# Five opening steps of an attention and gated-convolution kernel: order on TensorE, and which engine casts what when

## The chip, the cores and the metric

One core of one Trainium2 chip runs the program. The metric is device time in microseconds (us); lower is better. The engines are named as in the profile: PE is TensorE's matmul, PEld its weight load, DVE is VectorE, ACT is ScalarE, POOL is GpSimd, SP is the queue that issues nearly all DMAs.

## The reference, cut to what matters

Batch 8, 8 heads, 576 positions, head dimension 64. Attention is causal by blocks of 64; its output, 512 wide, goes through a causal depthwise convolution of five taps, a sigmoid gate, and two 512 by 512 projections.

```python
scores = scale * np.matmul(q, k.transpose(0, 1, 3, 2))
mask = (pos[:, None] // 64) >= (pos[None, :] // 64)
attn = softmax(np.where(mask, scores, -1e9))
x = np.matmul(attn, v)            # heads laid side by side: 576 x 512
gate_pre = sum(conv_w[k] * x_shifted_by(4 - k) for k in range(5))
gate = 1.0 / (1.0 + np.exp(-gate_pre))
out = (gate * (x @ w_val)) @ w_out
```

All inputs and the output are float32 in HBM. The kernel computes in float16 with float32 accumulation, so each input is cast once on the chip.

## The kernel before

**Units of work.** The 64 (batch, head) pairs are taken two heads at a time: 32 steps, numbered p = 0 to 31, four to a batch. Of the 576 positions the first 512 are loaded per step; the last 64 of all heads of a batch (the "tail") are loaded and cast once for a batch. Names used below, with p a step and b a batch:

- `load_qk1(p)`, `load_v1(p)`, `load_tails(b)`, `load_vtail(b)`: DMAs into float32 staging tiles (`qks`, `vs`, `tlst`, `vtst`; four buffers each for the first two).
- `cast_qk(p)` (L130), `cast_v(p)` (L135), `cast_tails(b)` (L116), `cast_vtail(b)` (L119): casts to float16, on POOL after step 0.
- `trans(p)`: eight TensorE transposes of the cast Q and K (L156) into PSUM bank 2, then one DVE copy (L167) into `qkT`. This is the input transpose; step p needs the result of `trans(p)`.
- `s_tile(p, t)` for t = 0, 1, 2: score matmuls into one of two PSUM tiles named `S`, then an exponential on ACT (L190) into `pt`.
- `s_last(b)`: the scores of the tails of one batch, with an exponential on ACT (L200).
- `mask(p)`: two POOL memsets on `pt` (L206, L208) that zero what causality forbids; it needs the exponential of `s_tile(p, 2)`.
- `av(p, h, bank)`: 15 matmuls of `pt` by V for head h; `norm(p, h, bank)`: reciprocal and multiply on DVE (L237, L238) into `x16`. `avs` is `av`, `norm` for head 0 and then for head 1.
- `xtrans(p)`: five transposes of `x16` (L252), the output transpose, and a DVE copy (L254) into `xt`.
- `conv(n)`: 80 small matmuls and three tanh activations (L275, L278); `val`, `out_tile`: the two projections.
- `trans_tails(b)`: transposes of the cast tail (L142) and a DVE copy (L145).
- `cast_w_out(f)` (L394), `permute_w_out(x)`: the output weights are cast in two halves at steps 7 and 8 and permuted by small matmuls at steps 9 to 11.

**Order.** The order on each engine is the order of the statements, written out by hand; nothing reorders it. An engine takes its instructions strictly in that order and waits on semaphores for the others. Steps 0 to 4 are one loop (attention only), steps 5 to 31 a second loop, which adds the convolution and the projections of a step five earlier. In each step `loads(p)` is issued first (Q and K of step p + 4, V of step p + 3), then `casts(p)` (Q and K of step p + 1, V of step p), then the scores.

Two of the details that are touched: at step 6 the cast of batch 2's tail comes not with the other casts but after `mask(6)`, and from step 9 on `casts(p)` casts Q and K up to two steps ahead.

Of the kernel before, what the change touches and what calls it, by code (L numbers as in the profile page):

```python
# [10 lines left out]
def kernel(  # L11
# [10 lines left out]
    nc = tc.nc  # L22
# [5 lines left out]
    B, H, SEQ, D = q.shape  # L28
    NP = B * H // 2
    out2d = out.rearrange("b s n -> (b s) n")  # L30

    def mm(out, lhsT, rhs, start=True, stop=True):
        nc.tensor.matmul(out=out, lhsT=lhsT, rhs=rhs, start=start, stop=stop,  # L33
                         skip_group_check=True)
# [10 lines left out]
    def const(shape, dt, tag):  # L45
        return cpool.tile(shape, dt, tag=tag, name=tag)
# [7 lines left out]
    w_st2 = const([128, 4, 512], fp32, "w_st2")  # L54
    w16 = const([128, 4, 512], fp16, "w16")
# [16 lines left out]
    def gbank(i=None):  # L72
        if i is None:
            i = ring[0] % 4
            ring[0] += 1
        return GT[i]
# [3 lines left out]
    qk16, tl16, qkT, gv = {}, {}, {}, {}  # L80
# [32 lines left out]
    def cast_tails(b, eng):  # L113
        t = p2.tile([128, 8, 64], fp16, tag="tl16", name="tl16")
        tl16[b] = t
        eng.tensor_copy(out=t[0:128, 0:8, 0:64], in_=tl_st.pop(b)[0:128, 0:8, 0:64])  # L116

    def cast_vtail(b):
        nc.gpsimd.tensor_copy(out=v16t[b % 2][0:128, 0:8, 0:64], in_=vtst[b % 2][0:128])  # L119

    def cast_qk(p, first=False):
        t = p3.tile([128, 4, 4, 64], fp16, tag="qk16", name="qk16")
        qk16[p] = t
        s = qk_st.pop(p).rearrange("p i h (n d) -> p (i h) n d", n=4)
        o = t[0:128].rearrange("p n e d -> p e n d")
        if first:
            nc.vector.tensor_copy(out=o[:, 0:2], in_=s[:, 0:2])
            nc.vector.tensor_copy(out=o[:, 2:4], in_=s[:, 2:4])
        else:
            nc.gpsimd.tensor_copy(out=o, in_=s)  # L130

    def cast_v(p):
        b, g = divmod(p, 4)
        s = v_st.pop(p)
        nc.gpsimd.tensor_copy(out=v16s[p % NV][0:128, 0:4, 0:2, 0:64], in_=s)  # L135
# [13 lines left out]
    def trans(p, bank=None):  # L149
        t = qk16.pop(p)  # L150
        banks = (2, 0) if p == 0 else (bank, bank)
        rr = [GT[i][0:128].bitcast(fp16) for i in banks]
        for i in range(2):
            for c in range(4):
                o = 512 * i + 128 * c
                nc.tensor.transpose(out=rr[i][:, o:o + 128], in_=t[0:128, c, 2 * i:2 * i + 2, 0:64],  # L156
                                    identity=ident16[0:128, 0:128])
        src = [r.rearrange("p (i n s) -> p i s n", i=2, n=4) for r in rr]
        if p == 0:
            o = [const([128, 512], fp16, f"qk0_{i}")[0:128] for i in range(2)]  # L160
            nc.scalar.copy(out=o[0].rearrange("p (s n) -> p s n", n=4), in_=src[0][:, 0])
            nc.vector.tensor_copy(out=o[1].rearrange("p (s n) -> p s n", n=4), in_=src[1][:, 1])
            qkT[p] = o
        else:
            o = p3.tile([128, 2, 512], fp16, tag="qkT", name="qkT")
            qkT[p] = [o[0:128, i] for i in range(2)]
            nc.vector.tensor_copy(out=o[0:128].rearrange("p i (s n) -> p i s n", n=4), in_=src[0])  # L167
# [36 lines left out]
    def mask(p):  # L204
        pt = pts[p % NPT]
        nc.gpsimd.memset(  # L206
            pt[64:128, 0:2, 0:1536].rearrange("p h (t s) -> p h t s", t=3)[:, :, :, 0:64], 0.0)
        nc.gpsimd.memset(pt[64:128, 0:2, 896:960], 0.0)  # L208
# [6 lines left out]
    def av(p, h, bank):  # L215
        b, g = divmod(p, 4)
        pt = pts[p % NPT]
        vv = v16s[p % NV]
        r = gbank(bank)
        for i in range(5):  # L220
            for j in range(i + 1):
                if j == 4:
                    o = 64 * (4 * h + g)
                    l = pt4[b % 2][0:128].rearrange("p a s -> p (a s)")[:, o:o + 128]
                    w = v16t[b % 2][0:128, 2 * g + h, 0:65]
                else:
                    o = 1280 + 64 * j if i == 4 else off[j] + 128 * i
                    l = pt[0:128, h, o:o + 128]
                    w = vv[0:128, j, h, 0:65]
                mm(r[0:128, 65 * i:65 * i + 65], l, w, start=(j == 0), stop=(j == i))  # L230

    def norm(p, h, bank):
        if h == 0:
            x16[p] = p3.tile([128, 5, 2, 64], fp16, tag="x16", name="x16")
        O = GT[bank][0:128, 0:325].rearrange("p (i d) -> p i d", d=65)
        rc = p2.tile([128, 5, 1], fp32, tag="rc", name="rc")
        nc.vector.reciprocal(out=rc[0:128], in_=O[:, :, 64:65])  # L237
        nc.vector.tensor_tensor(  # L238
            out=x16[p][0:128, 0:5, h, 0:64], in0=O[:, :, 0:64],
            in1=rc[0:128].to_broadcast([128, 5, 64]), op=ALU.mult)  # L240

    def avs(p, banks):
        for h in range(2):
            av(p, h, banks[h])
            norm(p, h, banks[h])
# [106 lines left out]
    def warm(n, bank=1):  # L352
        for _ in range(n):
            mm(GT[bank][0:128, 0:512], wz[0:128, 0:128], wz[0:128])
# [36 lines left out]
            scalar1=0.5, scalar2=None, op0=ALU.mult)  # L391

    def cast_w_out(f):
        nc.gpsimd.tensor_copy(out=w16[0:128, 2 * f:2 * f + 2, 0:512],  # L394
                              in_=w_st2[0:128, 2 * f:2 * f + 2, 0:512])


    T_LOAD = {{1: 0, 2: 4, 3: 7}.get(b, 4 * b - 6): b for b in range(1, B)}
    T_CAST = {{1: 3, 2: 6, 3: 9}.get(b, 4 * b - 4): b for b in range(1, B)}
    T_TRANS = {{1: 3, 2: 7, 3: 10}.get(b, 4 * b - 4): b for b in range(1, B)}  # L400
    T_LAST = {{0: 0, 1: 4, 2: 8, 3: 12}.get(b, 4 * b - 2): b for b in range(B)}

# [16 lines left out]

    def casts(p):  # L420
        for i in (p + 1, p + 2):
            if i < NP and i not in qkT and i not in qk16 and (p >= 9 or i == p + 1):
                cast_qk(i)
        cast_v(p)
        if p % 4 == 0:
            cast_vtail(p // 4)
        if p in T_CAST and p != 6:
            cast_tails(T_CAST[p], nc.gpsimd)

    def mask_and_casts(p):  # L430
        mask(p)
        if p == 6:
            cast_tails(T_CAST[p], nc.gpsimd)
        if p in (7, 8):
            cast_w_out(p - 7)

    outs = []

# [11 lines left out]
    for p in range(LAG):  # L450
        loads(p)
        casts(p)
        s_tile(p, 0)
        s_tile(p, 1)
        if p == 0:
            warm(2)
            trans_tails(0, 0)
            s_tile(0, 2)
            mask(0)
            trans(1, 2)  # L460
            warm(2)
            s_last(0)
            conv_weights()
            continue
        if p > 1:
            xtrans(p - 2, 3)
        av(p - 1, 0, 0)
        norm(p - 1, 0, 0)
        av(p - 1, 1, 1)
        trans(p + 1, 2)  # L470
        norm(p - 1, 1, 1)
        s_tile(p, 2)
        mask_and_casts(p)
        if p == 1:
            warm(2, 3)
        if p in T_TRANS:
            trans_tails(T_TRANS[p], 0)
        if p == 4:
            s_last(1)

    for p in range(LAG, NP):
        gs = p - LAG
        cv = gs % 2 == 0
        early = p < 12
        h = gs - 1
        loads(p)
        casts(p)
        if p == 6:
            scale_w_val(0)
            scale_w_val(1)  # L490
        s_tile(p, 0)
        s_tile(p, 1)
        if p == LAG:
            xtrans(p - 2, 3)
        avs(p - 1, (0, 1) if cv else (1, 0))
        if p < NP - 1:
            trans(p + 1, 2)
        if not early:
            out(3)
        elif gs > 0:  # L500
            val(h // 2, 2 * (h % 2), 3)
        s_tile(p, 2)
        mask_and_casts(p)
        if p in T_LAST:
            s_last(T_LAST[p])
        if cv:
            conv(gs // 2, (0, 1), early)
        xtrans(p - 1, 2 if cv else 0)
        if gs > 0:
            if not early:  # L510
                val(h // 2, 2 * (h % 2), 3)
            val(h // 2, 2 * (h % 2) + 1, 3 if early and cv else 1 if early else 0 if cv else 2)
            if h % 2 == 1:
                complete(h // 2)
        if p == 6:
            scale_w_val(2)
            scale_w_val(3)
        if 9 <= p <= 11:
            permute_w_out({9: 0, 10: 1, 11: 3}[p], 2)
        if p == 10:  # L520
            permute_w_out(2, 3)
        if p in T_TRANS:
            trans_tails(T_TRANS[p], 2 if cv else 0 if early else 1)
# [47 lines left out]
```

## Time and profile before

| what | value |
|---|---|
| median of 13 runs | 198.33 us (197.55 to 200.39) |
| the profiled execution, its time | 197.85 us |
| its span, first to last instruction | 196.1 us |
| PE busy | 180.6 us, 92% |
| ACT busy | 137.8 us, 70% |
| DVE busy | 131.7 us, 67% |
| POOL busy | 82.9 us, 42% |
| granted TensorE clock | 1.00 |
| HBM traffic over the span | 203 GB/s |

The table is of one profiled execution; the span leaves out 1.75 us that the execution's own time has around it. Busy shares are averages over the whole span. The kernel has two regimes: up to about 55 us PE has holes, and from then to about 176 us it has none to speak of. The row of POOL looks light, but a queue that is idle half the time can still hand over each piece late.

### The profile page before, as it was taken

How to read it: one execution, taken by the hardware profiler on the slowest of the kernel's cores; microseconds unless marked ns; L12 is line 12 of the kernel's file. 1: busy time of each engine (PE TensorE's matmuls, PEld its weight loads, DVE VectorE, ACT ScalarE, POOL GpSimd, SP SyncE). 2: the span in 40 equal slices, each digit the busy share in tenths (PEclk: the TensorE clock that was granted, in tenths of full speed). 3: DMA queues.
4: the chain of work that ended last, by engine and by line, in shares of the span. 5: the costliest groups of instructions: out<-in, count | busy, mean ns of one | idle time of the engine just before them, and what ended most of it. 6: DMA issues, size and time to landing. Idle time of an engine off the chain costs nothing.

```text
span 196.1 us, 8701 instructions
## 1 busy us (share of the span) xinstructions
PE 180.6 (92%) x3700; PEld 123.2 (63%) x3700; DVE 131.7 (67%) x287; ACT 137.8 (70%) x191; POOL 82.9 (42%) x168
## 2 busy tenths in 40 slices
PE   3897878869899999999999999999999999999992
PEld 0474665656576577677667776767767676755550
DVE  5378778958668586768677768687776867542451
ACT  0777788647688888877887788887888797545321
POOL 7274775156944644455434543464445422100000
PEclk9999999999999999999999999999999999999999
DMA  6999999999999567778797688868774111144355
GB/s 167 268 284 263 249 322 315 219 264 233 294 198 274 165 201 198 210 224 238 202 261 233 188 241 226 231 193 245 219 216 110 57 57 57 59 159 155 130 207 214
DMA packets 70337, 40.43 MB, mean 206 GB/s; under 512 B 48149, under 2 KB 64789, under 8 KB 70298
## 3 DMA queue, kind: packets, MB, share of 16 engines
q1 hardware_dynamic: 68288, 39.07, 72.5%
q10 hardware_dynamic: 2010, 0.80, 1.8%
q8 instruction: 29, 0.48, 1.1%
q14 instruction: 10, 0.08, 0.2%
HBM read 30.42 MB, written 9.44 MB: 203 GB/s over the span
## 4 chain that ended last, share of the span: by engine, by line
PE 79%; DMA 10%; DVE 3%; POOL 2%; ACT 1%; issue 1%; SPq 1%; ACTq 0%; POOLq 0%; DVEq 0%
PE G L33 48%; PE S L33 18%; PE G L156 7%; DMA qks<-in_k_dram 6%; PE G L252 5%; DMA tlst<-in_k_dram 3%; DVE qkT L167 2%; POOL qk L130 2%; DMA vs<-in_v_dram 1%; PE G L142 1%; ACT L324 1%; POOL w L394 1%; DVE xt L254 0%; DVE gv L292 0%; SPq L95 0%
## 5 line engine op out<-in xcount | busy, mean ns | idle before, releaser
L190 ACT ACTIVATE pt<-S 128x1024 f16<-128x1024 f32 x96 | 94.9, 1024 | 23.4 <-PE S L33 21.1
L206 POOL MEMSET pt<- 64x384 f16 x32 | 13.2, 413 | 77.9 <-ACT pt L190 77.9
L167 DVE COPY qkT<-G 128x1024 f16<-128x1024 f16 x31 | 37.7, 1216 | 4.1 <-PE G L156 4.0
L33 PE MATMUL G<-xt,w_val 128*128 128x288 f16 x256 | 38.7, 286 | 0.4 <-issue 0.4
L292 DVE SCALAR_TENSOR_TENSOR gv<-th,G 128x288 f16<-128x288 f32 x64 | 28.2, 452 | 13.1 <-PE G L33 11.5
L33 PE MATMUL G<-w_out,gv 128*128 128x512 f16 x144 | 36.5, 379 | 0.0
L33 PEld LDWEIGHTS <-pt 128*128 128x128 f16 x960 | 31.5, 97 | 7.3 <-issue 5.1
L33 PE MATMUL G<-v,pt 128*128 128x65 f16 x896 | 34.0, 194 | 1.3 <-issue 0.8
L130 POOL CAST qk<-qks 128x1024 f16<-128x1024 f32 x31 | 32.3, 1043 | 5.0 <-DMA qks<-in_k_dram 3.3
L314 ACT COPY osb<-G 128x512 f32<-128x512 f32 x31 | 18.2, 587 | 22.2 <-PE G L33 19.5
L238 DVE TENSOR_TENSOR x<-G,rc 128x320 f16<-128x320 f32 x64 | 31.4, 491 | 2.2
L33 PE MATMUL S<-qkT 64*128 64x512 f16 (+1 forms) x248 | 28.7, 301 | 3.3 <-DVE qkT L167 1.9
L33 PEld LDWEIGHTS <-qkT 64*128 64x128 f16 x496 | 16.2, 94 | 23.7 <-issue 16.3
L33 PEld LDWEIGHTS <-w_val 128*128 128x128 f16 x256 | 23.9, 98 | 8.0 <-issue 0.6
L254 DVE COPY xt<-G 128x576 f16<-128x576 f16 x32 | 14.6, 457 | 15.1 <-PE G L252 14.8
L156 PE MATMUL G<-ident,qk 128*128 128x128 f16 x256 | 20.1, 222 | 4.6 <-POOL qk L130 2.7
L237 DVE RECIPROCAL rc<-G 128x5 f32<-128x5 f32 x64 | 12.1, 189 | 17.8 <-PE G L33 17.6
L135 POOL CAST v<-vs 128x512 f16<-128x512 f32 x32 | 20.7, 648 | 0.7 <-DMA vs<-in_v_dram 0.5
L33 PEld LDWEIGHTS <-gv 128*128 128x128 f16 x144 | 12.9, 98 | 9.9
L156 PEld LDWEIGHTS <-qk 128*128 128x128 f16 x256 | 15.1, 99 | 6.1 <-POOL qk L130 3.1
L33 PE MATMUL G<-xt,DG 32*32 32x288 f16 x640 | 16.9, 288 | 0.0
L33 PE MATMUL S<-xt,DG 32*32 32x288 f16 x640 | 16.7, 287 | 0.0
(58 smaller groups left out, 147.1 us busy)
## 6 DMA issues: line engine op xcount, KB each, us to landing
out_dram<-osb SPq DMA_DIRECT2D x35, 256.0 KB, 2.4
qks<-in_q_dram SPq DMA_DIRECT2D x32, 256.0 KB, 4.2
qks<-in_k_dram SPq DMA_DIRECT2D x31, 256.0 KB, 4.4
vs<-in_v_dram SPq DMA_DIRECT2D x62, 128.0 KB, 4.5
tlst<-in_q_dram SPq DMA_DIRECT2D x8, 128.0 KB, 4.5
vtst<-in_v_dram SPq DMA_DIRECT2D x8, 128.0 KB, 4.6
w_st<-in_moe_w_val_dram SPq DMA_DIRECT2D x2, 512.0 KB, 6.1
w_st<-in_moe_w_out_dram SPq DMA_DIRECT2D x2, 512.0 KB, 6.2
```

The lines of the kernel that those rows point to most:

```text
L33: nc.tensor.matmul(out=out, lhsT=lhsT, rhs=rhs, start=start, stop=stop, skip_group_check=True)
L130: nc.gpsimd.tensor_copy(out=o, in_=s)
L135: nc.gpsimd.tensor_copy(out=v16s[p % NV][0:128, 0:4, 0:2, 0:64], in_=s)
L156: nc.tensor.transpose(out=rr[i][:, o:o + 128], in_=t[0:128, c, 2 * i:2 * i + 2, 0:64], identity=ident16[0:128, 0:128])
L167: nc.vector.tensor_copy(out=o[0:128].rearrange("p i (s n) -> p i s n", n=4), in_=src[0])
L190: nc.scalar.activation(out=pts[p % NPT][0:128, 0:2, 512 * t:512 * t + 512], in_=s[0:128, 0:2, 0:512], func=AF.Exp, bias=0.0, scale=0.125)
L206: nc.gpsimd.memset(pt[64:128, 0:2, 0:1536].rearrange("p h (t s) -> p h t s", t=3)[:, :, :, 0:64], 0.0)
L237: nc.vector.reciprocal(out=rc[0:128], in_=O[:, :, 64:65])
L238: nc.vector.tensor_tensor(out=x16[p][0:128, 0:5, h, 0:64], in0=O[:, :, 0:64], in1=rc[0:128].to_broadcast([128, 5, 64]), op=ALU.mult)
L254: nc.vector.tensor_copy(out=xts[b % NX][0:128, g, 4:4 + SEQ], in_=r[:, 0:SEQ])
L292: nc.vector.scalar_tensor_tensor(out=gv[u][0:128, x, bi, hf, 0:288], in0=t[0:128, x, 0:288], scalar=1.0, in1=r[0:128, 0:288], op0=ALU.add, ...
L314: nc.scalar.copy(out=o[0:128], in_=r[0:128, 0:512])
```

## The change

In the first loop the order on PE becomes: scores 0 and 1, `trans(p + 1)`, `xtrans(p - 2)`, `av` and `norm` of both heads, score 2. Before, `trans(p + 1)` stood after both `av`. The second loop keeps its order.

The two halves of the output weights are cast by ACT instead of POOL, at the same place in steps 7 and 8. The cast of batch 2's tail goes from after `mask(6)` to the end of `casts(7)`. The cast of Q and K of step 11 goes from `casts(9)` to after `mask(9)`.

```diff
     def cast_w_out(f):
-        nc.gpsimd.tensor_copy(out=w16[0:128, 2 * f:2 * f + 2, 0:512],
-                              in_=w_st2[0:128, 2 * f:2 * f + 2, 0:512])
+        nc.scalar.copy(out=w16[0:128, 2 * f:2 * f + 2, 0:512],
+                       in_=w_st2[0:128, 2 * f:2 * f + 2, 0:512])
...
-    T_CAST = {{1: 3, 2: 6, 3: 9}.get(b, 4 * b - 4): b for b in range(1, B)}
+    T_CAST = {{1: 3, 2: 7, 3: 9}.get(b, 4 * b - 4): b for b in range(1, B)}
...
     def casts(p):
         for i in (p + 1, p + 2):
-            if i < NP and i not in qkT and i not in qk16 and (p >= 9 or i == p + 1):
+            if i < NP and i not in qkT and i not in qk16 and (p > 9 or i == p + 1):
                 cast_qk(i)
         cast_v(p)
         if p % 4 == 0:
             cast_vtail(p // 4)
-        if p in T_CAST and p != 6:
+        if p in T_CAST:
             cast_tails(T_CAST[p], nc.gpsimd)
-
-    def mask_and_casts(p):
-        mask(p)
-        if p == 6:
-            cast_tails(T_CAST[p], nc.gpsimd)
-        if p in (7, 8):
-            cast_w_out(p - 7)
...
# first loop, steps 1 to 4
+        trans(p + 1, 2)
         if p > 1:
             xtrans(p - 2, 3)
-        av(p - 1, 0, 0)
-        norm(p - 1, 0, 0)
-        av(p - 1, 1, 1)
-        trans(p + 1, 2)
-        norm(p - 1, 1, 1)
+        avs(p - 1, (0, 1))
         s_tile(p, 2)
-        mask_and_casts(p)
+        mask(p)
...
# second loop, steps 5 to 31
         s_tile(p, 2)
-        mask_and_casts(p)
+        mask(p)
+        if p == 9:
+            cast_qk(11)
+        if p in (7, 8):
+            cast_w_out(p - 7)
         if p in T_LAST:
             s_last(T_LAST[p])
```

## The prediction

> **What bounds the kernel now.** I looked first at busy time by stretch, from where TensorE (PE) starts to be full to where the last scores are done. Columns: stretch, length, then busy time and count for each engine.
>
> ```profile
> 55.30:176.00 120.70, 120.14 (x2585) 83.87 (x2585) 85.44 (x189) 94.30 (x133) 50.18 (x95) 1.00 0.66 185
> ```
>
> PE is busy 120.14 of 120.70 us. The change moves no matmul out of this stretch, so whatever time step 9 ends earlier or later should reach the end of the span one for one. Only PE's holes before 55 us are open.
>
> Next the timelines of steps 2 and 3, of POOL, PE and ACT (start, length, instruction; idle time before it and its releaser in brackets).
>
> ```profile
> 15.75 0.41 POOL L206 MEMSET pt<- 64x384 f16 x1 [1.72 <-ACT pt L190]
> 16.37 1.04 POOL L130 CAST qk<-qks 128x1024 f16<-128x1024 f32 x1
> 19.61 0.41 POOL L206 MEMSET pt<- 64x384 f16 x1 [1.63 <-ACT pt L190]
> ```
> ```profile
> 16.18 0.45 PE L252 MATMUL G<-ident,x 128*128 128x128 f16 x5
> 16.46 0.59 PE L33 MATMUL G<-v,pt 128*128 128x65 f16 x14
> 17.47 0.62 PE L156 MATMUL G<-ident,qk 128*128 128x128 f16 x8
> 18.02 0.28 PE L33 MATMUL S<-qkT 64*128 64x256 f16 x2
> 19.41 0.61 PE L33 MATMUL S<-qkT 64*128 64x512 f16 x6 [0.98 <-DVE qkT L167]
> ```
> ```profile
> 18.46 1.02 ACT L190 ACTIVATE pt<-S 128x1024 f16<-128x1024 f32 x1 [0.54 <-PE S L33]
> ```
>
> The bracket at 19.41 shows what a reorder could remove: the next scores wait 0.98 us for the copy behind the input transpose. But the other rows close a ring of the same length: mask at 15.75, cast 16.37, transpose 17.47, third score 18.02, its exponential 18.46, next mask 19.61: 3.86 us. The cast stands behind the mask in POOL's queue, so POOL's 1.7 us of idling before a mask is no slack: it waits for its own product to come round. The output transpose and both `av` (16.18 to 17.47) lie beside the mask and cast, outside the ring.
>
> Last, POOL and PE in step 7, and then step 9:
>
> ```profile
> 37.47 0.41 POOL L206 MEMSET pt<- 64x384 f16 x1 [3.48 <-ACT pt L190]
> 39.16 0.62 POOL L116 CAST tl<-tlst 128x512 f16<-128x512 f32 x1 [1.15 <-DMA tlst<-in_k_dram]
> 39.72 1.05 POOL L130 CAST qk<-qks 128x1024 f16<-128x1024 f32 x1
> 49.52 1.04 POOL L394 CAST w<-w_st 128x1024 f16<-128x1024 f32 x1
> ```
> ```profile
> 40.82 0.62 PE L156 MATMUL G<-ident,qk 128*128 128x128 f16 x8 [1.80 <-POOL qk L130]
> 51.61 0.62 PE L156 MATMUL G<-ident,qk 128*128 128x128 f16 x8 [0.87 <-POOL qk L130]
> ```
>
> POOL stands at the tail cast until its DMA lands (the chain of waits has that transfer from 32.43 to 39.02), with the cast for step 8 queued behind it. That step's K was issued at 29.6 and took 6.4 us by the tile's view, so it was there at 36.0. At step 9 a weight cast stands ahead of an input cast.
>
> [...] two exponentials of that size take 1.94, one 1.02. [...] here a 1.80 us hole left it at 1.00.
>
> **Part 1, the order in steps 1 to 4.** Moved ahead on PE: eight transposes; on DVE their 1.23 us copy, now ahead of the `xtrans` copy and of head 0's `norm`. No DMA is in it. Gone: the PE waits for `qkT`, 1.9 us in three. New: `trans` reaches PE before its cast, and behind it wait `xtrans`, `av`, `norm` and the third score, all of which had run meanwhile. So the ring takes in `xtrans` and both `av`. From the rows:
>
> - mask to cast 0.62, cast to transpose 1.10 (as before)
> - transpose to next 0.55; `xtrans` 0.29 (20.03 to 20.32); both `av` 0.92 (12.69 to 13.62 is 0.93)
> - third score to exponential 0.48, exponential to mask 1.14
>
> Sum 5.10 against 3.86: **+1.24 a step**. In step 1 the cast ends at 12.87, so the transpose starts at 12.92, `av` at 13.47, the third score at 14.40, mask 1 at 16.01 instead of 15.75: +0.26. Steps 2 to 4 follow: 21.11, 26.21, 31.31. The last was 27.44: **+3.87 us** at step 5. The new wait for the transpose in steps 2 to 4 is some 1.8 us.
>
> Does that reach step 7? Steps 5 and 6 are not paced by transfers: K of step 7 landed at 31.7 (the chain of waits), before its cast could run in either order. They keep their lengths: mask 6 goes from 37.47 to 41.34. The loads need casts of earlier steps to free their buffers: Q and K of step 9 were issued at 35.85, the cast that frees them would end near 28. SP's stream stays as it is.
>
> **Part 2, the tail cast behind the step-8 cast.** With the mask at 41.34 the cast starts at 41.96 and its transpose at 43.06 instead of 40.82: +2.24. PE itself would be ready at 42.73 (38.86 plus 3.87). So 3.87 becomes 2.24, **-1.63**. Half of what part 1 loses was hidden in a wait that this edit takes away; alone, the edit would gain the same 1.63. The moved cast (0.62) then runs from about 43.5 and is needed at step 7's end, near 46.4: hidden.
>
> **Part 3, weight casts on ACT.** Step 7: 0.95 us go ahead of the tanh group (before: 43.29 to 44.54). Behind it wait the second score tile of step 8 and `av`, whose bank the last tanh frees: that tanh ends at 47.73 and `av` starts at 47.78 against 47.27, +0.51. The transpose after it had stood about 0.26 for POOL, which goes: **+0.25**. Step 8: the cast delays the tail's exponential (48.68) and with it the second score tile of step 9 by 0.95, in front of `av` and `trans`; in exchange the 1.03 us between `av`'s end (50.58) and the transpose (51.61) goes: **-0.06**. Unknown: how ACT's copy reads SBUF. Floor for the pair -0.6 (both hidden), ceiling +1.2; I take +0.2, from ACT's order above.
>
> **Part 4, the cast for step 11.** It now ends near 58.4 (old mask 9 at 54.30, shifted by 2.4, plus 0.62 and 1.04); its transpose comes near 59.2 (56.75 before). Zero, with 0.8 us of cover; without it PE would wait for the difference.
>
> **Sum.** +3.87 - 1.63 + 0.25 - 0.06 = **+2.4 us**. The profiled execution took 197.85 (span 196.1 plus 1.75), so 200.3 for its like; the median of the runs is 0.48 above it, 198.33, which gives **200.7**.
>
> Bounds: the ring per step between 1.0 and 1.4, giving 3.1 to 4.4; part 3 as above[...]. The case's own range is 199.3 to 202.2.
>
> **Rivals.**
>
> *Faster: POOL is not in the way.* If the cast for p + 1 were done when PE ends the second score tile of step p, the reorder would hide the copy: -1.9 for the three waits, -1.4 from the other edits, 195.0. For it: the 0.98 us wait, and POOL idle 58% of the span. Against it: in steps 2 and 3 the cast ends at 17.41 and 21.27, the transposes at 17.47 and 21.32 follow at once; after PE's second score (16.16) the cast has 1.25 us to go. It decides when the ring's growth falls under 0.48 a step (1.44 over three). Chance 0.10.
>
> *About the same: the transfers pace the opening anyway.* DMA is full up to 64 us. If step 8's inputs rather than POOL set the 40.82, all delay up to there would be free: about 198.3. Against it: K of step 8 had been there since 36.0. Chance 0.07.
>
> *Slower still: TensorE's clock halves in steps 2 to 4.* Those PE pieces in the ring (0.55, 0.29, 0.92, 0.4) would double, +2.2 on each of three steps: 207. Against it: holes of 1.8 us, as one that did no harm. Chance 0.04.
>
> **Chances and range.** The main case has 0.79. About 0.5% is what a measurement of this kernel can tell from no change. Slower by more: 0.84; faster by more: 0.11; within it: 0.05. The range 198.5 to 202.4 takes in the main case and half of the one beside zero.
>
> **What would show it.** Right: masks in steps 1 to 4 some 5.1 us apart; `trans` waiting 1.4 to 1.9 us for POOL L130 in each of steps 2 to 4, and no scores waiting for `qkT`; step 5 starting near 31.2 (27.37 before); the transpose of step 8 at about 43.1, without a tail cast ahead of its input cast; step 9's scores waiting 1 us longer for ACT; PE full from then on. Wrong: masks 3.9 us apart or closer, step 5 before 28, or a step 8 that starts no later than 44.5.

## The result, and the profile after

The changed kernel took a median of 203.07 us in 11 runs (201.22 to 207.63). The kernel before, now over 48 runs, had 199.86 (197.4 to 204.69); its first 13 runs had lain at the lower side of that. The ratio is **1.0179, 95% interval 1.0139 to 1.0219**: 1.8% slower. One per cent is about 2.0 us here, so that is some 3.6 us. Ratios here and below leave out slow executions, those more than 1.5% above the fastest of their kernel. The profiled execution of the changed kernel has a span of 201.6 us against 196.1.

First the page's slices: where PE is full, and at which clock. Each digit is one of 40 slices of the span. In the row of PE it is the busy share in tenths; PEclk is the granted clock in tenths.

```profile
PE   3896567989989999999999999999999999999992
PEclk9999886999999999999999999999999999999999
```

The second row was all nines before. Now slices 5 to 7 (some 20 to 35 us) are at 8, 8 and 6: the clock fell, and not late or at random but in steps 3 and 4. After the opening nothing changed, as PE's busy time shows (the second figure, after the length), over a stretch as long as the one shown of before and 5.5 us later:

```profile
60.79:181.50 120.71, 120.36 (x2569) 83.91 (x2568) 85.75 (x189) 94.48 (x134) 51.45 (x96) 1.00 0.63 179
```

PE is full as before, so what the opening lost stayed lost. The timeline of POOL in steps 2 to 5 (start, length, instruction; idle time before it and what ended it):

```profile
16.99 0.41 POOL L206 MEMSET pt<- 64x384 f16 x1 [1.95 <-ACT pt L190]
17.61 1.04 POOL L130 CAST qk<-qks 128x1024 f16<-128x1024 f32 x1
...
22.04 0.41 POOL L206 MEMSET pt<- 64x384 f16 x1 [2.82 <-ACT pt L190]
22.66 1.04 POOL L130 CAST qk<-qks 128x1024 f16<-128x1024 f32 x1
...
28.55 0.41 POOL L206 MEMSET pt<- 64x384 f16 x1 [3.73 <-ACT pt L190]
29.17 1.04 POOL L130 CAST qk<-qks 128x1024 f16<-128x1024 f32 x1
...
35.19 0.41 POOL L206 MEMSET pt<- 64x384 f16 x1 [3.85 <-ACT pt L190]
```

The masks are 5.05, 6.51 and 6.64 us apart, where they had been 3.86 to 3.92. The first of the three is the ring that the prediction drew (5.10). PE's timeline shows what the other two add. The first group is step 2, the second step 3, each from the input transpose to the third score tile:

```profile
18.71 0.62 PE L156 MATMUL G<-ident,qk 128*128 128x128 f16 x8 [1.39 <-POOL qk L130]
19.17 0.44 PE L252 MATMUL G<-ident,x 128*128 128x128 f16 x5
19.45 0.59 PE L33 MATMUL G<-v,pt 128*128 128x65 f16 x14
...
20.45 0.28 PE L33 MATMUL S<-qkT 64*128 64x256 f16 x2
...
23.75 1.04 PE L156 MATMUL G<-ident,qk 128*128 128x128 f16 x8 [1.39 <-POOL qk L130]
24.59 0.74 PE L252 MATMUL G<-ident,x 128*128 128x128 f16 x5
25.12 0.97 PE L33 MATMUL G<-v,pt 128*128 128x65 f16 x14
...
26.91 0.28 PE L33 MATMUL S<-qkT 64*128 64x256 f16 x2
```

Both steps wait the same 1.39 us for the cast. But in step 3 the same transposes take 1.04 us instead of 0.62, and the same `av` 0.97 instead of 0.59. From the start of the transposes to the third score tile it is 3.16 us instead of 1.74. The reason is the granted clock. It was at 0.50 from 23.52 to 26.94 and from 30.35 to 33.76 (the table of windows further down), two windows of 3.41 us, each of which covers the run of `trans`, `xtrans` and `av` of one step.

In step 7 the wait that had been 1.80 us is gone, and POOL takes the step-8 cast first, then V, then the tail:

```profile
44.83 1.04 POOL L130 CAST qk<-qks 128x1024 f16<-128x1024 f32 x1
45.81 0.81 POOL L135 CAST v<-vs 128x512 f16<-128x512 f32 x1
46.57 0.80 POOL L116 CAST tl<-tlst 128x512 f16<-128x512 f32 x1
```

In step 9 PE no longer waits for POOL, but for the exponential of the tail, which stands behind the second weight cast on ACT:

```profile
56.15 0.39 PE L33 MATMUL S<-qkT 64*128 64x384 f16 x4 [1.04 <-ACT pt L200]
```

The difference of the two profiled executions, mask by mask, in us:

| stretch | before | after | difference | predicted |
|---|---|---|---|---|
| start to mask 0 | 11.21 | 12.23 | +1.02 | 0 |
| step 1 | 4.54 | 4.76 | +0.22 | +0.26 |
| step 2 | 3.86 | 5.05 | +1.19 | +1.24 |
| step 3 | 3.91 | 6.51 | +2.60 | +1.19 |
| step 4 | 3.92 | 6.64 | +2.72 | +1.18 |
| step 5 | 4.14 | 4.14 | 0 | 0 |
| step 6 | 5.89 | 4.88 | -1.01 | 0 |
| step 7 | 6.04 | 4.56 | -1.48 | -1.63 |
| step 8 | 5.40 | 6.01 | +0.61 | +0.25 |
| step 9 | 5.39 | 5.30 | -0.09 | -0.06 |
| steps 10 to 13 | 20.99 | 20.78 | -0.21 | 0 |
| sum, mask 13 | 75.29 | 80.86 | +5.57 | +2.4 |

The first row belongs to no edit: the first K landed 5.57 us after the span's start instead of 4.57, which holds up everything behind it. Most of the gain in step 6 is the 0.84 us hole that PE had before 34.54 in the kernel before, in mid-`av` and with no semaphore that ends it; it was not there this time. The runs' difference, 3.6 us, is smaller than the 5.5 of this pair for such reasons.

### The profile page after: what moved, and what is told of

Same layout as the page of the kernel before. It is cut to its first block, busy times and chain, and to the rows that moved or that the text cites. A ratio compares the mean times of both kernels' runs of the same rounds, so it can differ in the third digit from the quotient of the medians.

```text
span 201.6 us, 8698 instructions
## 1 busy us (share of the span) xinstructions
PE 183.5 (91%) x3700; PEld 125.9 (62%) x3700; DVE 131.2 (65%) x287; ACT 139.2 (69%) x193; POOL 81.3 (40%) x166
## 4 chain that ended last, share of the span: by engine, by line
PE 76%; DMA 7%; DVE 7%; ACT 4%; POOL 2%; issue 2%; SPq 0%; ACTq 0%; POOLq 0%; DVEq 0%
PE G L33 47%; PE S L33 17%; PE G L156 6%; PE G L252 5%; DMA qks<-in_q_dram 3%; DMA qks<-in_k_dram 2%; DMA vtst<-in_v_dram 2%; ACT pt L190 2%; DVE qkT L167 2%; POOL qk L130 2%; DVE x L238 1%; DVE w_val L388 1%; PE G L142 1%; DVE gv L292 1%; DVE xt L254 1%
## 5 line engine op out<-in xcount | busy, mean ns | idle before, releaser
L190 ACT ACTIVATE pt<-S 128x1024 f16<-128x1024 f32 x96 | 94.6, 1024 | 26.8 <-PE S L33 24.5
L33 PEld LDWEIGHTS <-pt 128*128 128x128 f16 x960 | 33.1, 100 | 6.0 <-issue 3.5
L33 PE MATMUL G<-v,pt 128*128 128x65 f16 x896 | 35.4, 197 | 0.4 <-ACT th L278 0.2
L156 PE MATMUL G<-ident,qk 128*128 128x128 f16 x256 | 21.0, 227 | 6.7 <-POOL qk L130 4.3
L156 PEld LDWEIGHTS <-qk 128*128 128x128 f16 x256 | 15.6, 101 | 9.0 <-POOL qk L130 5.5
```

The lines of the kernel that those rows point to most:

```text
L190: nc.scalar.activation(out=pts[p % NPT][0:128, 0:2, 512 * t:512 * t + 512], in_=s[0:128, 0:2, 0:512], func=AF.Exp, bias=0.0, scale=0.125)
```

## The experiments

Theory A: the new order puts output transpose and attention output into the ring of mask, cast, transpose, score and exponential; the holes that this opens on PE lower the clock. Theory B: the weight casts on ACT are what costs. A third possibility is that the order is bad by itself, wherever the casts stand. All ratios are to runs of the kernel before on the same chip.

**The order alone.** The kernel before with the new first loop.

```diff
+        trans(p + 1, 2)
         if p > 1:
             xtrans(p - 2, 3)
-        av(p - 1, 0, 0)
-        norm(p - 1, 0, 0)
-        av(p - 1, 1, 1)
-        trans(p + 1, 2)
-        norm(p - 1, 1, 1)
+        avs(p - 1, (0, 1))
```

> The kernel before with the new order of steps 1 to 4 alone; all casts where they were. Theory A (the order puts the output transpose and attention output into POOL's mask-cast ring, and the holes it opens on PE let the clock fall to half for a window of 3.4 us or two): masks of steps 1 to 4 at least 5.0 us apart, 6.5 where the clock is at half; step 5 starts 4 to 7 us later than before; some 1.6 us of it are absorbed in the wait for the tail cast in step 7, so 1.5 to 4 us slower than the kernel before. Theory B (the loss of the changed kernel comes mostly from the weight casts on ACT): within 1 us of the kernel before.

Measured: 1.0199 (1.0144 to 1.0254) in 6 runs, so +4.0 us, at the upper end of what theory A gave. The masks are 5.05, 6.64 and 6.56 us apart in steps 2 to 4, with the clock at half in two windows again. Theory B is out: the whole loss is there with all casts in their old places.

**The casts alone.** The changed kernel with the first loop of before.

```diff
-        trans(p + 1, 2)
         if p > 1:
             xtrans(p - 2, 3)
-        avs(p - 1, (0, 1))
+        av(p - 1, 0, 0)
+        norm(p - 1, 0, 0)
+        av(p - 1, 1, 1)
+        trans(p + 1, 2)
+        norm(p - 1, 1, 1)
```

> The changed kernel with the old order of steps 1 to 4: only the casts are moved. Theory A: steps 1 to 4 as before (masks 3.9 us apart, clock 1.00), the 1.80 us wait of step 7 shrinks to about 0.2, 1.0 to 1.8 us faster than the kernel before. Theory B: slower than before, by up to 2 us, with PE waiting for ACT at steps 8 and 9.

Measured: 0.9938 (0.9907 to 0.9968), -1.2 us. The masks of steps 2 to 4 are 3.86, 3.92 and 3.91 apart, the wait in step 7 is 0.23 us, and one of 1.04 us for ACT stands in step 9. So the three cast edits together gain, and the change's two halves have opposite signs.

**Filler matmuls where PE waits.** The changed kernel; five matmuls on zeros that nothing reads.

```diff
+        if p > 1:
+            warm(5, 2)
         trans(p + 1, 2)
         if p > 1:
             xtrans(p - 2, 3)
```

> The changed kernel with five idle-time matmuls on zeros (1.1 us at full clock) ahead of the input transpose of steps 2 to 4, where PE waits 1.4 us for POOL; they add no work that anything needs. If the half clock is caused by the holes and costs 2.8 us: clock 1.00 throughout, masks 5.0 to 5.1 us apart in steps 2 to 4, and 2 to 3 us less than the changed kernel (so 0.5 to 2 us over the kernel before). If the clock is not what stretched steps 3 and 4 beyond 5.1 us: no gain over the changed kernel, or a loss of up to 1 us.

Measured: 1.0082 (1.0055 to 1.0108). Doing useless work took 2 us off the changed kernel, about the lower end of what was expected. The mean clock over an execution was 0.996 or more in 21 of 22 executions, against 0.973 to 0.992 in all those of the changed kernel. PE's timeline in step 3, at full clock again:

```profile
21.66 1.25 PE L33 MATMUL G<-wz 128*128 128x512 f16 x5
23.11 0.62 PE L156 MATMUL G<-ident,qk 128*128 128x128 f16 x8 [0.20 <-POOL qk L130]
23.57 0.44 PE L252 MATMUL G<-ident,x 128*128 128x128 f16 x5
```

The masks are 5.05, 5.10 and 5.11 us apart, as the ring's sum said. So of the 1.8%, about 1.0 is the clock, and 0.8 is the ring less the gain of the casts. What went with the lower clock can be read from PE's busy time in windows of 3.41 us, laid so that the clock changes only at their boundaries (in the changed kernel at 23.52, 26.94, 30.35 and 33.76). Columns: stretch, length, PE busy time and count, granted clock, DMA share, GB/s. Changed kernel:

```profile
16.69:20.11 3.42, 1.79 (x39) 1.00 1.11 219
20.11:23.52 3.41, 1.35 (x30) 1.00 0.98 233
23.52:26.94 3.42, 3.19 (x45) 0.50 1.09 301
26.94:30.35 3.41, 1.49 (x23) 1.00 1.11 333
30.35:33.76 3.41, 3.41 (x53) 0.50 1.11 327
```

With the filler:

```profile
16.71:20.12 3.41, 3.21 (x60) 1.00 1.15 203
20.12:23.53 3.41, 2.31 (x27) 1.00 1.13 247
23.53:26.95 3.42, 2.64 (x60) 1.00 1.08 303
```

Windows with 1.35 and 1.49 us of work (40% and 44%) are each followed by one at half clock; those with 1.79 us (52%) or more are not. The kernel before, where its 1.80 us hole lies:

```profile
39.56:42.97 3.41, 2.15 (x102) 1.00 1.05 261
```

The hole is longer than any of the changed kernel's, but it runs from 39.02 to 40.82, and a boundary at 39.56 cut it. That boundary is an estimate, counted back by 46 windows of 3.413 us from 196.58, where the trace of before has the clock falling to 0.50 behind the last instruction; in the changed kernel the fall at 201.02 lies 49 such windows behind 33.76. This window was 63% busy, the one before it 80% (2.73 of 3.41 us), and the clock held at 1.00. A window from 37.45 on would have caught the whole hole and been 43% busy (1.47 us). So in these traces it is the busy share of a window that tells, not the length of one hole. Where the boundaries lie differed from execution to execution: counted from the span's start the first half clock began at 23.52 in the changed kernel, at 23.18 with the order alone and at 25.79 with the cast ahead, which are not whole windows apart.

The same shows over many executions. One window at half clock takes about 0.009 off the mean clock of a run of 198 us, by an estimate from the 3.41 us at 0.50. In 48 of the 128 executions of the kernel before that ran beside these experiments the mean was 0.992 or less, but only in 4 of 22 with the casts alone and in 2 of 15 with the tail cast alone, which have no such hole in step 7. That the lost window lay at step 7 in those 48 is likely, but no trace shows one.

**Q and K cast a step earlier, out of the ring.** The changed kernel, where the cast for step p + 2 stands ahead of `mask(p)` in steps 1 to 3.

```diff
-            if i < NP and i not in qkT and i not in qk16 and (p > 9 or i == p + 1):
+            if i < NP and i not in qkT and i not in qk16 and (p in (1, 2, 3) or p > 9 or i == p + 1):
```

> The changed kernel with Q and K cast two steps ahead in steps 1 to 3, so that the cast stands ahead of the mask in POOL's queue and is out of the ring. Theory A: masks 3.5 to 4.0 us apart in steps 1 to 4, the input transpose waits under 0.3 us for POOL, clock 1.00, step 5 starts no later than before, and the whole is 1 to 2.5 us faster than the kernel before. Rival (it is the order on PE or DVE itself, or transfers, not the ring through POOL): steps of 4.5 us or more remain, and the whole is slower than before by 1 us or more.

Measured: 1.0054 (1.0021 to 1.0086), against theory A's forecast of a gain. Step 2 did as forecast (masks 3.59 us apart, no wait of the transpose for POOL), steps 3 and 4 did not (5.47 and 5.74). POOL's timeline in step 3:

```profile
22.80 1.04 POOL L130 CAST qk<-qks 128x1024 f16<-128x1024 f32 x1 [2.69 <-DMA qks<-in_k_dram]
23.78 0.62 POOL L135 CAST v<-vs 128x512 f16<-128x512 f32 x1
24.34 0.62 POOL L116 CAST tl<-tlst 128x512 f16<-128x512 f32 x1
```

and PE's:

```profile
25.02 0.40 PE L142 MATMUL G<-ident,tl 128*128 128x128 f16 x4 [3.06 <-POOL tl L116]
```

K of step 5 had not landed. POOL stood at its cast for 2.69 us, and the tail's cast behind it, which PE needed first, came late. It is the mistake of step 7 of the kernel before, made anew in step 3; the 3.06 us hole then brought a window of half clock:

```profile
22.38:25.79 3.41, 0.78 (x10) 1.00 1.03 303
25.79:29.20 3.41, 3.41 (x49) 0.50 1.06 321
```

**The same with the tail first.** In step 3 the casts of V and of the tail go ahead of the early cast; steps 1 and 2 stay as in the last run.

```diff
-            if i < NP and i not in qkT and i not in qk16 and (p > 9 or i == p + 1):
+            if i < NP and i not in qkT and i not in qk16 and (p in (1, 2) or p > 9 or i == p + 1):
...
         if p in T_CAST:
             cast_tails(T_CAST[p], nc.gpsimd)
+        if p == 3:
+            cast_qk(5)
```

> The new order with Q and K cast two steps ahead, as in the run before of that kind, but in step 3 the cast of batch 1's tail and of V stand ahead of the cast for step 5, whose K lands late. If the 3.06 us hole of that run was this one queue position: no hole over 1.1 us on PE in steps 2 to 4, clock 1.00 in most runs, masks 3.5 to 4.1 us apart, 0.5 to 2 us faster than the kernel before. If the new order costs by itself even with the cast out of the ring: slower than the kernel before by 0.5 us or more with the clock at 1.00.

Measured: **0.9901** (0.9871 to 0.9931), 2.0 us faster than the kernel before. The masks of steps 2 to 4 are 3.59, 4.41 and 3.39 us apart, and the largest hole on PE in these steps is 0.90 us. The new order itself is therefore no loss; the cast inside the ring was. The wait for the `qkT` copy, which the order was able to remove, is gone here too. Whether the order gains anything over the casts alone (0.9938) is not shown, since the intervals overlap. The profiled execution took 199.32 us, more than the median: its clock was at half from 66.24 to 69.65, far behind these steps, after a hole of 2.04 us at 62.93 that no semaphore explains.

**The tail cast alone.** The kernel before, with batch 2's tail cast at the end of `casts(7)`.

```diff
-    T_CAST = {{1: 3, 2: 6, 3: 9}.get(b, 4 * b - 4): b for b in range(1, B)}
+    T_CAST = {{1: 3, 2: 7, 3: 9}.get(b, 4 * b - 4): b for b in range(1, B)}
...
-        if p in T_CAST and p != 6:
+        if p in T_CAST:
...
-        if p == 6:
-            cast_tails(T_CAST[p], nc.gpsimd)
```

> The kernel before with the cast of batch 2's tail behind the casts of step 7, nothing else. The prediction's sum: 1.63 us faster, with the 1.80 us hole of step 7 shrinking to about 0.2 and the 0.87 us hole of step 9 staying. If transfers for step 8 take its place: 0 to 0.5 us faster, with a hole on a DMA in step 7.

Measured: 0.9946 (0.9907 to 0.9986), -1.1 us; the interval, -1.8 to -0.3, holds the predicted 1.63. The hole of step 7 is 0.36 us, that of step 9 stays at 0.86.

**The weight casts on ACT alone.** The kernel before with `nc.scalar.copy` in `cast_w_out`.

```diff
-        nc.gpsimd.tensor_copy(out=w16[0:128, 2 * f:2 * f + 2, 0:512],
-                              in_=w_st2[0:128, 2 * f:2 * f + 2, 0:512])
+        nc.scalar.copy(out=w16[0:128, 2 * f:2 * f + 2, 0:512],
+                       in_=w_st2[0:128, 2 * f:2 * f + 2, 0:512])
```

> The kernel before with the two weight casts on ACT, nothing else. The prediction's sum: 0.2 us slower (-0.6 to +1.2): the 0.87 us hole on POOL in step 9 goes and one of about 1 us on ACT ahead of step 9's second score tile comes in its place. If ACT's copy from SBUF takes much longer than 1.04 us: over 1.2 us slower.

Measured: 0.9996 (0.9965 to 1.0028): no difference. ACT's timeline at step 8:

```profile
48.04 1.02 ACT L190 ACTIVATE pt<-S 128x1024 f16<-128x1024 f32 x1 [0.67 <-PE S L33]
48.96 1.04 ACT L394 CAST w<-w_st 128x1024 f16<-128x1024 f32 x1
49.89 0.60 ACT L200 ACTIVATE pt<-S 128x512 f16<-128x512 f32 x1
```

The tail's exponential starts 0.93 us after the weight cast, and PE waits 1.04 us for it at 50.55, where 0.87 us for POOL had been. One wait was traded for another of its size.

**The weight casts behind the input casts, on POOL.** Old order; the other two cast edits as in the change.

```diff
-        nc.scalar.copy(out=w16[0:128, 2 * f:2 * f + 2, 0:512],
-                       in_=w_st2[0:128, 2 * f:2 * f + 2, 0:512])
+        nc.gpsimd.tensor_copy(out=w16[0:128, 2 * f:2 * f + 2, 0:512],
+                              in_=w_st2[0:128, 2 * f:2 * f + 2, 0:512])
...
         if p in T_CAST:
             cast_tails(T_CAST[p], nc.gpsimd)
+        if p in (7, 8):
+            cast_w_out(p - 7)
...
-        if p in (7, 8):
-            cast_w_out(p - 7)
```

> Old order; tail cast and cast for step 11 moved as in the change; the weight casts stay on POOL but stand behind the input casts of steps 7 and 8 instead of ahead of those of steps 8 and 9. If ACT's share of the change costs PE about 1 us in step 9 (as the wait for ACT in the run with the casts alone suggests): no PE hole over 0.3 us in steps 8 and 9, and 1.5 to 2.8 us faster than the kernel before, 0.3 to 1.3 faster than with the casts on ACT. If the ACT casts are free: the same as with the casts on ACT, about 1.2 us faster than the kernel before.

Measured: 0.9878 (0.9784 to 0.9972) in only 5 runs. The trace shows what it should: no hole on PE in steps 8 and 9 over 0.25 us, and a span of 193.9 us. The interval is too wide to tell it from the run with the casts on ACT.

**Both together.** The kernel with the tail first, and the weight casts on POOL at the end of `casts(7)` and `casts(8)`.

> The new order with the casts of steps 3 to 5 out of the ring (as in the run with the tail cast first), and the weight casts on POOL behind the input casts. If the two gains add: the hole of 1.04 us on ACT ahead of step 9's second score tile is gone, clock 1.00 in most runs, and the ratio to the kernel before is 0.98 to 0.99, at least 0.4 us below that of the same kernel with the weight casts on ACT (0.990). If something else sets step 9 once that hole is gone (a landing of step 10's or 11's K): the same as with the casts on ACT.

Measured: **0.9877** (0.9838 to 0.9915), median 196.32 in 13 runs, 2.4 us under the kernel before and the lowest median of all. The hole on ACT is gone. That it beats the same kernel with the casts on ACT (0.9901) is not shown: the intervals overlap.

## Why the prediction was right or wrong

The direction and the ring were right, the size was not: +2.4 us were forecast, some 3.6 came, and the median lies above the range. The step that failed is the clock. The prediction left it out of its sum and priced it as a separate rival with a chance of 0.04; the filler shows that it cost 2 us. With the clock held by the filler, the trace has mask 9 2.30 us later than before, counted from mask 0, for a forecast of 2.43; the runs with the filler gave +1.6 us (1.1 to 2.1), somewhat under the sum.

**Part 1, the ring: right, and a term of 2 us was still missing.** Step 2 grew by 1.19 for the predicted 1.24, step 1 by 0.22 for 0.26. With the clock held by the filler, steps 3 and 4 came to 5.10 and 5.11 against the sum's 5.10. What failed is the step "here a 1.80 us hole left it at 1.00" (the granted clock), from which the prediction gave the clock a chance of 0.04. It judged by the length of a hole, and that this length decides was shown by no trace. In the changed kernel windows that were 40% and 44% busy (1.35 and 1.49 of 3.41 us) were each followed by half clock, and no hole in them was longer than 1.39 us. The hole of 1.80 us was also a weak witness, since by that estimate a boundary happened to cut it. The prediction could have had the share: its own ring held about 2.7 us of PE work in 5.1 us (scores 0.6, `trans` 0.55, `xtrans` 0.29, `av` 0.92, third score 0.4), near one half on average, and a window that catches the hole holds less. At which share the clock falls, no profile that it had could tell.

The price of that rival was too high in turn. That the clock would be halved was its author's assumption; the trace of before, with 1.00 over the whole span, shows no such thing. It forecast 2.2 us on each of three steps; 1.4 and 1.5 us on two were measured. Step 2 kept its clock, as the window before it was 94% busy (3.22 of 3.41 us). In step 3 the half clock ended at 26.94, just after the third score began, and the pieces before it grew by 1.42 us (1.74 to 3.16), so they did not quite double, and the third score hardly grew.

The 1.8 us wait forecast for the transpose was 1.39; the rest of the hole stood ahead of the second score tile (0.90 and 0.53), which waited for ACT's exponential (L190) to free its PSUM buffer. It lies before the cast is done and costs nothing more.

**Part 2, the tail: right.** -1.48 in the pair of profiles, -1.1 alone in the runs, for -1.63. One reading was slightly off: PE was busy to 39.02, not 38.86, so it would have been ready at 42.89, which is still ahead of 43.06. The moved cast ran hidden at 46.57, as said.

**Part 3, weights on ACT: right.** +0.2 (range -0.6 to +1.2) was forecast, and the edit alone measured -0.1 us (-0.7 to +0.6). ACT's copy took 1.04 us, and the instruction behind it started 0.93 to 0.94 us after the copy's start, for the 0.95 that the prediction added. The 0.95 was shown by no trace. In that of before two exponentials of 128x1024 took 1.94 and one 1.02, so the second added 0.92; with this the forecast for steps 7 and 8 would have been an estimated +0.22 and -0.09 in place of +0.25 and -0.06. In the traces of the casts alone and of the weight casts alone step 8 grew by 0.21 for the predicted 0.25. In that of the changed kernel it grew by 0.61; there `conv` also waited 0.35 us for DVE's `norm`, a queue that the prediction did not follow past step 4.

**Part 4: right.** The cast for step 11 ran behind mask 9, from 60.70 on, and PE had no wait for POOL in step 10.

**The hole of step 6: it mostly recurs, but not with one size.** It was 0.84 us before 34.54 and absent in the changed kernel's profiled execution. In the experiments' traces it stands at the same place of step 6 in eight of nine, with 0.17 to 1.38 us. What causes it is shown by no run. The lower end of the main case's range, 199.3, allowed for it to go away.

**The rivals.** "POOL is not in the way" was refuted by the 1.39 us waits. That transfers pace the opening was refuted by the order alone costing 4.0 us. "The clock halves" came on top of the main case, as an effect of it, where the prediction had treated the two as exclusive; that is why the sum came out too low. Its base moved as well: the ratio 1.0179 on the 198.33 of the first runs would be 201.9, inside the range. So of the 2.4 us between the forecast 200.7 and the measured 203.07, about half is the change and half the base.

## What to carry to other kernels

Before moving an instruction forward on one engine, follow the ring through all engines that its input closes: work that lay beside the ring can come to lie in it, and an engine that is idle half the time can still be a link of it (POOL, 42% busy over the span). In a queue that works in the order of its statements put the cast or copy whose data lands last behind those that are needed first; that fixed step 7 of the old kernel (a hole of 1.80 us on PE became 0.36) and step 3 of the new order alike (3.06 became at most 0.90). When a forecast opens holes on TensorE, work out the busy share of every stretch of 3.4 us, wherever it may begin, and price the half clock as part of that case: in the changed kernel 1.35 and 1.49 us of work in windows of 3.41 us were each followed by one at 0.50.

## What the runs showed of the hardware

- In the eleven traces, counted in windows of 3.41 us from some 10 us after the span's start, every window in which PE was busy for 41% or less was followed by one at 0.50 (0.78 us with the cast ahead of the tail, 1.12 with the order alone, 1.35 in the changed kernel, 1.37 with the tail first). None with 52% or more was (1.79 in the changed kernel, 1.87 with the cast ahead, 1.93 with the weights on ACT). Between the two both happened: 1.49 us (44%) was followed by half clock in the changed kernel and with the order alone, while at the end of the program 1.42 us (42%, filler) and 1.51 us (44%, cast ahead) were not. No hole in those windows of the changed kernel exceeded 1.39 us.
- While the program had work for PE, the half clock lasted one window each time: from 23.52 to 26.94 and from 30.35 to 33.76 in the changed kernel, from 23.18 to 26.59 and from 30.00 to 33.42 with the order alone, from 25.79 to 29.20 with the cast ahead, from 66.24 to 69.65 with the tail first.
- Five filler matmuls on zeros in each of three steps took 2 us off the changed kernel (ratio 1.0082 against 1.0179, mean clock 0.996 or more in 21 of 22 executions against 0.973 to 0.992).
- The first K landed 4.57 us after the span's start in one execution and 5.57 us in another, with the same statements ahead of it. In the eleven traces mask 0 began between 10.86 and 12.23 us.
